# TensorE in program order through a first attention with no weight conversion beside it, and value blocks moved in the load queue

## The chip, the cores and the metric

One core of one Trainium2 chip runs the whole program. The metric is the device time of one execution in microseconds (us). Times of different kernels are compared only through runs of the same rounds on the same chip.

## The reference, cut to what matters

```python
# q, k, v: (4, 8, 768, 64) float32; two weights: 512 x 2048 and 2048 x 512
def _attn_ref(q, k, v):                       # block 32, window 16
    k_sum = k.reshape(B, H, nb, 32, D).max(axis=3)     # one key per block
    v_sum = v.reshape(B, H, nb, 32, D).mean(axis=3)    # one value per block
    # softmax over near keys (|i - j| < 16) and all block keys (+ log 32)
    ...
    return np.matmul(a, np.concatenate([v, v_sum], axis=2))

def _moe_ref(x, w_ch1, w_ch2):                # x: (4, 768, 512)
    mixed = np.real(np.fft.fft(np.fft.fft(x, axis=1), axis=2))
    u = x + mixed
    un = (u - u.mean(-1)) / np.sqrt(u.var(-1) + 1e-6)
    return u + np.maximum(un @ w_ch1, 0.0) @ w_ch2
```

Each of the four batches goes through attention (four pairs of heads), Fourier mixing, a norm, a hidden layer and an output layer. The two products with the weights are most of the work.

## The kernel before, where the change and the argument touch it

The weights arrive as 64-bit words, and VectorE and ScalarE turn them into float32 on the chip, one half matrix at a time. Each of the 16 matrices (w1 and w2, eight each) is needed first in batch 0, so all conversion lies in batch 0's time. The list `plan` says in which order matrices are converted, and from which stage on each may begin (`None` is at once, `fold` and `mx` are stages of the Fourier mixing).

```python
plan = [(1, 0, None), (1, 1, ("fold", 0)), (1, 2, ("mx", 0)), (2, 0, ("mx", 0)), (1, 3, ("h", 0, 0)), ...]

def convert(piece, dst):                      # one half of a matrix
    load_raw(i + 3)                           # loads run three pieces ahead
    nc.vector.tensor_scalar(out=ex, in0=high, ...bitwise_and)       # 2 of these, 0.42 us each
    nc.vector.tensor_scalar(out=man, in0=high, ...bitwise_and)
    nc.scalar.activation(out=ex, ...); nc.scalar.activation(out=tmp[:, 1, :], ...)
    nc.vector.scalar_tensor_tensor(out=ex, in0=high, ..., in1=ex, ...)   # 2 of these
    nc.vector.scalar_tensor_tensor(out=tmp[:, 1, :], in0=low, ..., in1=tmp[:, 1, :], ...)
    tt(dst, tmp[:, 1, :], tmp[:, 0, :], ALU.mult)                   # VectorE
    ...
def make(f, j):                               # two halves, then sums of quarters
    ...
    if f == 1:
        _left_sums(tt, ...)                   # 4 VectorE sums, for products of seven instead of eight
    else:
        to, wv = to[:, 0:4], wv[:, 0:4]       # w2: no sums in batch 0; batch 1 makes them on its first load
```

Block sums of the values are made from loads of their own, on GpSimd (`gtt`) or, for batch 1, on VectorE (`tt`). A load of the next half of a batch is issued together with the values of every second pair.

```python
def block_sums(b, gg):                        # 4 heads
    ...                                       # 4 loads of 192 KB
    add = tt if b == 1 else gtt
    add(raw[0], raw[0], raw[1], ADD)          # 6 operations on GpSimd, 4 on VectorE
    ...
def load_values(b, g):
    if g % 2 and following(b, g, 1):
        block_sums(*divmod((b * NP + g + 1) // 2, NP // 2))
    ...
def get_w2(b, j):                             # from batch 1 on
    if b == 1:
        fetch(out=w[:, 0:4], in_=dw2[j][:, 0:4])
        _right_sums(tt, lambda i: w[:, i])    # 4 VectorE sums
        fetch(out=dw2[j][:, 1:7], in_=w[:, 1:7])
```

In the output layer batch 0 uses plain products, the others seven products of half size in place of eight. In the fold at the start of the Fourier mixing, `keep_busy` lets TensorE multiply the fold's own tiles, which is meant to keep its clock up.

## Time and profile before

| | before |
|---|---|
| median of 3 runs (range) | 847.06 us (846.79 to 847.75) |
| profiled span, granted clock | 846.1 us, 0.988 |
| first hidden matmul, first output matmuls of batch 0 | 103.07, 152.44 us |
| second hidden half of batch 0 starts | 203.96 us |
| output of batch 0's second half | 63.42 us |

Two views of the kernel before: VectorE from the end of the norms (97.23 us) to the last w2 matrix of the first output (159.87 us), in which the columns are the stretch, its length, then busy us (and instructions) of PE, PEld, DVE, ACT and POOL, the granted clock, the DMA share and GB/s; and TensorE's waits from the first hidden matmul to the second half (engine, line and tile, what it waited for, us in total, times, longest).

```profile
97.23:159.87 62.64, 57.59 (x582) 33.99 (x580) 52.68 (x104) 41.27 (x79) 6.36 (x6) 1.00 0.81 232
```

### The profile page before, as it was taken

What the parts mean: (1) busy time and instruction counts of PE and PEld (TensorE: products, weight loads), DVE (VectorE), ACT (ScalarE), POOL (GpSimd) and SP (SyncE); (2) the same over time, 40 slices, a digit from 0 to 9 for tenths busy, and PEclk for the clock granted to TensorE, in tenths of its full rate; (3) what the DMA queues carried; (4) which work ended last, traced back from release to release, by engine and by line L of the source; (5) the groups of instructions that cost most, each with busy time, mean ns of one, the idle gap of its engine ahead of it and who ended that gap; (6) DMA issues with size and microseconds to landing.
All of it is one profiled execution on the core that took longest, in us unless ns stands there. A gap on an engine that the chain in (4) does not pass through costs nothing.

```text
span 846.1 us, 14497 instructions
## 1 busy us (share of the span) xinstructions
PE 813.9 (96%) x6006; PEld 569.1 (67%) x6006; DVE 479.4 (57%) x1115; ACT 230.5 (27%) x473; POOL 36.3 (4%) x44
## 2 busy tenths in 40 slices
PE   6979988999999999999999999999999999999997
PEld 5857655545556555787667875688667885786586
DVE  2588996986966443544357943443337952532352
ACT  3524756542721113122232104120321012101100
POOL 3200011003000200001000000000000000000000
PEclk9969999999999999999999999999999999999999
DMA  9997594979523274454843236403411326205001
GB/s 220 230 274 164 166 232 171 289 235 298 187 78 131 75 277 131 116 112 158 239 106 100 71 134 215 115 21 82 167 60 54 113 64 247 88 1 217 1 27 53
DMA packets 102858, 120.94 MB, mean 143 GB/s; under 512 B 50592, under 2 KB 83584, under 8 KB 102784
## 3 DMA queue, kind: packets, MB, share of 16 engines
q1 hardware_dynamic: 102240, 119.77, 48.6%
q8 instruction: 49, 0.80, 0.4%
q10 hardware_dynamic: 544, 0.17, 0.1%
q14 instruction: 25, 0.20, 0.1%
HBM read 95.80 MB, written 24.12 MB: 142 GB/s over the span
## 4 chain that ended last, share of the span: by engine, by line
PE 79%; DVE 10%; ACT 5%; DMA 3%; issue 1%; SPq 0%; ACTq 0%; DVEq 0%
PE hx L1101 18%; PE ox L1167 13%; PE o L1142 9%; PE hz L1101 9%; PE oz L1167 7%; PE hy L1101 4%; PE y L1014 3%; PE oy L1167 3%; DVE x L560 2%; PE sc L735 2%; PE mx L963 1%; ACT qt L678 1%; ACT kt L678 1%; PE sc L695 1%; PE unt L1079 1%
## 5 line engine op out<-in xcount | busy, mean ns | idle before, releaser
L1101 PE MATMUL hx<-u,w 128*128 128x384 f32 x512 | 186.1, 492 | 8.8 <-ACT h L1111 6.2
L1101 PEld LDWEIGHTS hx<-u,w 128*128 128x128 f32 x512 | 94.4, 190 | 75.5 <-ACT h L1111 9.4
L1101 PE MATMUL hz<-u,w 128*128 128x384 f32 x256 | 93.2, 486 | 0.0
L1142 PE MATMUL o<-w,h 128*128 128x512 f32 x192 | 84.9, 595 | 0.0
L1101 PEld LDWEIGHTS hz<-u,w 128*128 128x128 f32 x256 | 48.6, 190 | 33.9 <-ACT h L1118 0.2
L1167 PE MATMUL ox<-w,s 128*128 128x256 f32 x288 | 69.0, 381 | 0.4 <-DVE x L560 0.3
L1167 PE MATMUL oz<-w,s 128*128 128x256 f32 x288 | 68.7, 379 | 0.0
L1167 PE MATMUL ox<-w,h 128*128 128x256 f32 x288 | 66.9, 380 | 0.0
L1142 PEld LDWEIGHTS o<-w,h 128*128 128x128 f32 x192 | 35.7, 190 | 41.9 <-issue 39.9
L560 DVE TENSOR_TENSOR x<-ox,x 128x256 f32<-128x256 f32 x72 | 30.3, 423 | 55.7 <-PE ox L1167 55.7
L1167 PEld LDWEIGHTS ox<-w,h 128*128 128x128 f32 x288 | 54.4, 190 | 8.3
L1167 PEld LDWEIGHTS ox<-w,s 128*128 128x128 f32 x288 | 53.9, 190 | 8.4 <-DVE x L560 1.2
L1167 PEld LDWEIGHTS oz<-w,s 128*128 128x128 f32 x288 | 54.4, 190 | 7.2
L560 DVE TENSOR_TENSOR h<-hx,h 128x384 f32<-128x384 f32 x32 | 17.8, 556 | 71.3 <-PE hx L1101 71.3
L560 DVE TENSOR_TENSOR h<-hy,h 128x384 f32<-128x384 f32 x32 | 17.8, 556 | 57.2 <-PE hy L1101 54.0
L1111 ACT COPY h<-hx 128x384 f32<-128x384 f32 x32 | 15.3, 478 | 121.7 <-PE hx L1101 110.0
L1101 PE MATMUL hy<-u,w 128*128 128x384 f32 x128 | 46.5, 486 | 0.0
L1127 ACT ACTIVATE h<-hx 128x384 f32<-128x384 f32 x32 | 15.7, 491 | 79.3 <-PE hx L1101 79.3
L1014 PE MATMUL y<-fs,fold 128*128 128x193 f32 x192 | 37.1, 336 | 0.0
L679 DVE TENSOR_REDUCE km<-kt 128x24 f32<-128x768 f32 x16 | 15.2, 951 | 37.7 <-ACT kt L678 24.6
L1014 PEld LDWEIGHTS y<-fs,fold 128*128 128x128 f32 x192 | 31.1, 189 | 7.4 <-issue 6.0
L1101 PEld LDWEIGHTS hy<-u,w 128*128 128x128 f32 x128 | 24.3, 190 | 17.0
(125 smaller groups left out, 1104.1 us busy)
## 6 DMA issues: line engine op xcount, KB each, us to landing
w<-dw SPq DMA_DIRECT2D x40, 896.0 KB, 5.2
words<-in_moe_w_ch_dram SPq DMA_DIRECT2D x32, 512.0 KB, 6.5
vw<-in_v_dram SPq DMA_DIRECT2D x47, 192.0 KB, 5.7
dw<-w SPq DMA_DIRECT2D x8, 896.0 KB, 6.9
kn<-in_k_dram SPq DMA_DIRECT2D x16, 384.0 KB, 4.9
qn<-in_q_dram SPq DMA_DIRECT2D x16, 384.0 KB, 5.7
vb<-in_v_dram SPq DMA_DIRECT2D x32, 192.0 KB, 5.6
out_dram<-x SPq DMA_DIRECT2D x24, 256.0 KB, 2.5
```

The costliest lines, as they stand in the source:

```text
L560: nc.vector.tensor_tensor(out=out, in0=in0, in1=in1, op=op)
L678: nc.scalar.copy(out=dst[D * e:D * (e + 1), s:S:2], in_=ps[D * s:D * (s + 1)])
L679: nc.vector.tensor_reduce(out=km[:, 0:nb], in_=kt[:, W:W + S].rearrange("p (n f) -> p n f", f=BLOCK), op=ALU.max, axis=AX.X)
L695: nc.tensor.matmul(ps[e][0:WK, n - n0, :], kt[rows, QB * n:QB * n + WK], qt[rows, QB * n:QB * (n + 1)], start=True, stop=True)
L735: nc.tensor.matmul(ps[h][r:r + 64, i, :], kt[rows, o:o + 64], qt[rows, o:o + BLOCK], start=True, stop=True)
L963: nc.tensor.matmul(out, y[:, g], table, start=True, stop=last, skip_group_check=True)
L1014: nc.tensor.matmul(y, fgs[par][:, st, P * g:P * (g + 1)], fs[par][:, g % 2, st, :], start=(st == 0), stop=(st == HT - 1))
L1101: nc.tensor.matmul(ps, w[:, a, kk, :], u[:, r, kk, :], start=start and kk == 0, stop=stop and kk == 1, skip_group_check=True)
L1111: nc.scalar.copy(out=c11, in_=X)
L1127: nc.scalar.activation(out=c21, in_=X, func=AF.Relu)
L1142: nc.tensor.matmul(ps, h[:, n, hf, P * t:P * (t + 1)], wt[2, b, j][:, 2 * hf:2 * hf + 2, :], start=(n, hf) == (0, 0), stop=(n, hf) == (NC ...
L1167: nc.tensor.matmul(ps, left[a][:, n, :], wt[2, b, j][:, r, :], start=start and n == 0, stop=stop and n == NC - 1, skip_group_check=True)
```

## The change

The intent: TensorE's first attention should run without waits. Its instructions keep the order of the program; warm-up matmuls run before the first keys land; pair 0's blocks get loads of half the size; the blocks of pairs 2 and 3 are loaded behind the keys of pair 3; no weight is converted in the attention; ScalarE takes copies of the fold. Beside this, the second half of batch 0's output becomes seven products, and batch 1's first block sums go to GpSimd.

```diff
-    plan = [(1, 0, None), (1, 1, ("fold", 0)), (1, 2, ("mx", 0)), ...
+    plan = [(1, 0, ("fold", 0)), (1, 1, ("mx", 0)), (1, 2, ("mx", 0)), ...
-        add = tt if b == 1 else gtt
+        add = tt if (b, gg) == (1, 1) else gtt
...
-        if g % 2 and following(b, g, 1):
+        if g % 2 and following(b, g, 1) and (b, g) not in ((0, 1), (1, 1)):
             block_sums(...)
...                                            # gen_attention, after pair 0's values
+            if (b, g) == (0, 0):
+                block_sums(0, 1)
+                load_raw(2)
...                                            # make, get_w2, gen_out
-        else:
+        elif j < NC:
             to, wv = to[:, 0:4], wv[:, 0:4]
+        else:
+            _right_sums(tt, lambda i: wv[:, i])
-        if b == 1:
+        if b == 1 and j < NC:
             fetch(out=w[:, 0:4], in_=dw2[j][:, 0:4])
-        if b == 0:
+        if (b, c) == (0, 0):
...                                            # fold: three copies from VectorE to ScalarE
-            nc.vector.tensor_copy(out=zq[:, par], in_=zw[:, :, Q])
+            nc.scalar.copy(out=zq[:, par], in_=zw[:, :, Q])
...
+    for i in range(2):
+        nc.tensor.matmul(ps, zeros[:, 512:640], zeros[:, 0:512], start=True, stop=True)
...
-    drive((first(attn, 6), 1, 0))
+    with tc.manual_schedule(engines={mybir.EngineType.PE}):
+        drive((first(attn, 6), 1, 0))
+    block_sums(1, 1)                           # behind the Fourier mixing of batch 0
```

(Cut: the mask of 32 KB for one of 384 KB, the split of pair 0's and 1's blocks, details of the value loads.)

## The prediction

> **What bounds the kernel now.** I read the page first: TensorE is busy 96% of the span, and the chain that ended last is 79% PE, 10% DVE, 5% ACT, 3% DMA. So most of the span is matmul time, which this change touches in one place only. What can be won lies where TensorE waits or runs at half clock, so I asked for stretches of the first 105 us, then the timeline of the end of the first attention. In each stretch the columns are length, then busy us (and instructions) of PE, PEld, DVE, ACT and POOL, then the granted clock, the DMA share and GB/s.
>
> ```profile
> 12.50:15.00 2.50, 1.50 (x22) 0.74 (x19) 2.37 (x3) 1.35 (x4) 2.34 (x3) 1.00 1.29 214
> 15.00:17.50 2.50, 0.57 (x4) 0.36 (x5) 1.50 (x2) 0.16 (x1) 1.52 (x3) 0.87 1.15 276
> ...
> 45.00:50.00 5.00, 5.00 (x41) 3.30 (x39) 3.13 (x6) 1.92 (x2) 0.00 (x0) 0.76 1.05 401
> 50.00:54.00 4.00, 3.65 (x50) 2.75 (x48) 2.87 (x6) 0.87 (x2) 0.00 (x0) 0.50 1.09 344
> 54.00:58.00 4.00, 0.00 (x0) 0.00 (x0) 4.00 (x7) 0.00 (x0) 0.13 (x1) 0.50 1.36 159
> ```
>
> See three things: TensorE starves at 14 to 17 us, DMA is full (share over 1) all along, and the last pair runs at clock 0.50. The timeline tells who is waited for.
>
> ```profile
> 16.73 0.57 PE L709 MATMUL vs<-vbs,sel 96*32 96x64 f32 x4 [2.73 <-POOL vbs L563]
> 17.51 2.83 PE L668 MATMUL qk<-ident,kn 128*64 128x128 f32 x24 [0.20 <-DMA kn<-in_k_dram]
> ...
> 41.12 0.63 ACT L860 ACTIVATE words<-words 128x512 f32<-128x512 int32 x1 [0.26 <-DVE words L858]
> ...
> 54.92 0.65 DVE L864 SCALAR_TENSOR_TENSOR words<-words 128x512 f32<-128x512 uint32 x1
> 55.48 0.55 DVE L560 TENSOR_TENSOR x<-av,rec 128x384 f32<-128x384 f32 x1
> 55.95 0.68 DVE L560 TENSOR_TENSOR w<-words 128x512 f32<-128x512 f32 x1
> 56.55 1.75 DVE L560 TENSOR_TENSOR fold<-x 128x1536 f32<-128x1536 f32 x1
> 58.35 4.24 PE L952 MATMUL busy<-fold,ident 128*128 128x512 f32 x6 [4.38 <-DVE fold L560]
> ```
>
> Block sums on POOL and the second pair's keys end the first stall. Weight conversion (`words`, `w`) sits in VectorE's queue between the last pair and the fold, and in ScalarE's queue among the last pair's copies. After that TensorE is busy 0.9 to 1.0, but VectorE, converting weights, is busy 35.4 of 40 us from 60 to 100 and 47.1 of 56.9 us from 103 to 160.
>
> **What the Trainium skill says.** (1) "TensorE: Matmul & The Clock Gate", Part 1: half clock when cold, full after some 3.4 us of sustained work. The trace agrees: 0.50 from 47.55 to 61.2 us, and a 24-matmul transpose group takes 2.83 us at the start, 1.53 us at 27.23. (2) "SBUF — State Buffer", two separate sides: a VectorE operation with two SBUF inputs and a GpSimd operation that reads SBUF exclude each other. I take it as the price of moving sums to GpSimd; no line above isolates it. (3) "DMA: Bandwidth & Descriptors", small descriptors: they are slow. The trace agrees: a 288 KB block of `vw` in 256-byte rows lands in some 1.4 us, 512 KB of weights in 1.3 to 2.3.
>
> **The change part by part.** For what moves I compared the order of instructions on each engine in both programs.
>
> *Start.* Warm-up matmuls before the keys land (4.62 us): 48 transposing matmuls of pair 0 took 2.83 + 2.80 us; at full clock some 3.0. The keys' arrival and the free-running clock window leave about 1 us of that. The mask shrinks from 384 to 32 KB and pair 0's value blocks from 768 to 384 KB, so 736 KB fewer lie before pair 1's keys: at 0.2 to 0.25 MB/us, 3 to 3.7 us. They should land near 14 us, not 17.4. POOL's sums start with the blocks (10.1 to near 7.8 us) and end near 14.3, and the matmul that needs them now follows the key transposes. Pair 1's scores start near 19.5 instead of 23.03: **3.5 us**.
>
> *A new wait.* The blocks of pairs 2 and 3 now come behind the keys of pair 3. Counting landings as before (2 us per 384 KB of keys, 2.6 per 768 KB of blocks), they land near 31 us, and POOL's sums took 6.5 us: ready near 36. In the new TensorE order everything of pair 3 stands behind that matmul (before: 36.67 us). So the 3.5 us shrink to **about 0.5** here, with TensorE idle some 3 us.
>
> *The last pair.* Before, from 36.67 to the last `av` at 53.97 took 17.3 us, half of it at half clock and with `words` activations between copies. In the new order: transposes 3, `av` 1.6, scores 3.9, ScalarE's value copy and last exponential 2, last mask and `av` 1.5, waits about 1: 13 us, plus up to 3 if the clock falls in the idle gap. End near 50: **4 us** gained.
>
> *Fold.* Removed between the last `av` and the fold: two word operations and one product (0.6 us apart each, partly under the `x` writes): 1.3 us. Inside the fold, four `w` sums (0.35 apart) and six copies go away or to ScalarE: 2 us. The first half gains 5.6 us (62.37 to 56.8), the second 7.8. TensorE then runs `y` and `mx` back to back (idle 0.8 us of 25 before), so 5.6 is what passes: hidden layer at 97.4 instead of 103.07.
>
> *Conversion given back.* One w1 matrix costs 6.3 us of VectorE: per half 2 x 0.335 + 3 x 0.60 = 2.47 us by start-to-start times, plus four sums of 0.34. About 5.8 us of the first one was paid within the attention and now comes after it; the value sums of batch 1's first half (3 us) leave VectorE. Before, the last w2 matrix that the first output tile needs was ready at 159.87, when TensorE wanted it. By adding the new VectorE order from the norms on (38.6 us conversion, 20 us other, 3 us waits) I get 152 to 154, so the gain there is 6 to 8 us: **7**. VectorE has the room because before it idled some 10 us waiting for TensorE.
>
> *Output of batch 0's second half as seven products.* Rows removed: 96 of 128x512, 42.0 us. Added: 168 of 128x256 at 1.73/8 = 0.216 us: 36.3. Net 5.7 at best. Batch 1 does just this already and is the better measure:
>
> ```profile
> 240.36:303.78 63.42, 63.42 (x242) 36.59 (x241) 37.66 (x103) 8.73 (x24) 4.99 (x5) 1.00 0.29 97
> 441.11:500.93 59.82, 59.25 (x314) 50.13 (x313) 45.88 (x126) 8.23 (x22) 0.00 (x0) 1.00 0.30 80
> ```
>
> 3.6 us less for the stage; I take **3**, since only 5.2 us of output matmuls now stand before the `y` that needs the fold (8 in batch 1). The 16 added w2 sums (6.8 us of VectorE) come while the hidden layer runs (24.6 busy of 36.4) and should just fit. Batch 1 loses the same sums and four stores: **1**, as the chain passed through one such load and sum at 391 to 399 us.
>
> Sum: 7 + 3 + 1 = 11: 847 - 11 = 836.
>
> **The rivals.** *VectorE becomes the bound at 60 to 160 us.* Every weight is one place later; if copies and rectifiers queue behind it, TensorE waits 1.1 to 1.5 us at a time on hidden copies, as before (6.2 us in five waits). For: busy 35.4 of 40. Against: one matrix is 6 us, and the fold is 7.8 earlier. It would leave 3 us at the front: 840 to 843. *The late blocks cost more than the early keys give.* For: DMA is full, and the sums take 6.5 us on POOL in series. Against: before, pair 3 began no earlier for other reasons. With a cold clock behind it, 2 us less: 838 to 840. *Pair 3 runs warm and without a gap*: attention ends at 46.5, and the w2 matrices come at 150: 830 to 832. *All hidden*: the attention's gain is taken back by transfers of tables; they land by 53.4 us, so this is unlikely.
>
> **Range and chances.** The front holds the doubt: 3 to 11 us. The other 4 us are likely to 1.5. So 836, 8 times in 10 within 829 to 843. Faster by 2% means under 830.1: only if pair 3 and the conversion both go well, 0.14. Slower by 2% would take a stall of 28 us that nothing shows: 0.01.
>
> **What would show it.** Right: `sc` of pair 1 near 19.5; `vs` of pair 2 waits for POOL near 36; last `av` at 48.5 to 51.5; first hidden matmul at 95 to 99; the output stage 3 us shorter; everything after 310 us the same, shifted. Wrong: `hx` waiting on VectorE's `w` or long on ScalarE copies between 100 and 155, the last `av` later than 52, a cold clock past 61 us, or a gap before the batch-0 output because w2 sums are late.

## More of the kernel before

```profile
PE hx L1101 <- ACT h L1111: 3.9, 3, 1.5
PE av L772 <- DVE vs L560: 1.2, 1, 1.2
PE hx L1101 <- DVE h L560: 0.9, 1, 0.9
```

VectorE is busy 52.68 of 62.64 us, the rest is waiting.

## The result

| | before | after |
|---|---|---|
| median (range), 4 runs each | 846.92 us (846.19 to 847.75) | 846.27 us (845.34 to 848.04) |
| ratio after/before, 95% interval | | 0.9994 (0.9976 to 1.0013): the same |
| profiled span, granted clock | 846.1, 0.988 | 844.2, 0.994 |

A ratio here and below is the mean time of one kernel's runs over the mean of the other's of the same rounds, so it is not quite the ratio of the medians. The changed kernel ran three rounds more on another chip beside later experiments: 845.77 us, 0.9985 (0.9962 to 1.0009). The prediction of 836 us, with a range of 829 to 843, was wrong.

Where the time went is seen by the starts of stages on TensorE, read from both traces:

| stage starts at (us) | before | after | gained so far | gained as predicted |
|---|---|---|---|---|
| scores of pair 1 | 23.03 | 20.54 | 2.5 | 3.5 |
| last `av` of the attention ends | 53.97 | 51.42 | 2.6 | 4 |
| first hidden matmul | 103.07 | 97.63 | 5.4 | 5.6 |
| second hidden half of batch 0 | 203.96 | 206.23 | -2.3 | 7 |
| output of the second half | 240.36 | 242.63 | -2.3 | 7 |
| first hidden matmul of batch 1 | 303.78 | 301.89 | 1.9 | 10 |
| first output of batch 1 | 349.36 | 349.98 | -0.6 | 10 or 11 |
| end | 846.14 | 844.25 | 1.9 | 11 |

At the first hidden matmul the gain is nearly what was foreseen (some 2.2 us of it is work that only moved behind this point, see below; the norms end 4.2 us earlier). Two stages took it back: 7.7 us between 97 and 206 us, and 2.5 us in batch 1's first hidden half. The 2.5 us between the last two rows are gained in four later stages, 0.4 to 0.8 us in each; no run looks into them. The same two views of the changed kernel (its norms end at 92.98 us, the last w2 matrix is ready at 162.68), and the waits from its first hidden matmul to the second half:

```profile
92.98:162.68 69.70, 63.24 (x596) 37.24 (x596) 62.68 (x124) 42.84 (x82) 6.58 (x6) 0.98 0.87 237
```

```profile
PE hx L1111 <- DVE h L560: 3.2, 1, 3.2
PE av L778 <- DVE vs L560: 1.7, 1, 1.7
PE hx L1111 <- ACT h L1121: 1.2, 1, 1.2
PE o L1152 <- DVE w L560: 0.9, 1, 0.9
```

The stretch is 69.70 us long, not 62.64; VectorE is busy 62.68 of it. TensorE now waits for VectorE, 5.8 us in all, where it waited 2.1 us for VectorE and 3.9 for ScalarE. The timeline (start, us, engine, line, operation, out<-in, shape, count, idle time before it and what ended that) shows what VectorE did before the longest wait:

```profile
127.03 4.97 POOL L563 TENSOR_TENSOR vb_None<-vb_None,vb_None 96x512 f32<-96x512 f32 x3 [75.40 <-DMA vb_None<-in_v_dram]
...
129.38 1.49 DVE L864 TENSOR_SCALAR words<-words 128x512 int32<-128x512 int32 x1
130.78 1.50 DVE L865 TENSOR_SCALAR words<-words 128x512 int32<-128x512 int32 x1
...
135.59 1.56 PE L1111 MATMUL hx<-u,w 128*128 128x384 f32 x4 [3.16 <-DVE h L560]
```

Two word operations take 1.49 and 1.50 us while GpSimd adds blocks. The same operation takes 0.42 us elsewhere. The sum into `h` stands behind them in VectorE's queue, and TensorE waits 3.16 us for it.

The 7.7 us are not all waiting, though. TensorE from its first hidden matmul to the second half, before and after (columns as above):

```profile
103.07:203.96 100.89, 94.83 (x773) 50.60 (x771) 85.88 (x168) 53.48 (x99) 12.91 (x12) 1.00 0.83 243
97.63:206.23 108.60, 101.29 (x797) 54.46 (x791) 95.80 (x188) 55.82 (x105) 14.89 (x12) 0.98 0.84 240
```

Its idle time grew from 6.1 to 7.3 us; the other 6.5 us it is busy. Three things in the two traces make up 6.2 of them. Transposes and block scores of batch 1's attention, which took 2.2 us right before the first hidden matmul (100.92 to 103.07 us), now come right after it. The scores of one pair come in two groups some 6 us apart: 48 matmuls alone take as long as 96 together (1.59 us at 118.71, 1.60 at 169.00), and with the block scores this costs 2.4 us. And after the wait of 3.16 us the clock reads 0.50 from 137 to 140 us, which costs 1.6. The program fixes TensorE's order in the first attention only; why it came out otherwise here, no run tests. So the time at which the last w2 matrix is ready is the better measure of VectorE's queue.

The second loss, in batch 1, reads so:

```profile
309.96 1.55 DVE L560 TENSOR_TENSOR w<-w 128x256 f32<-128x256 f32 x4 [2.88 <-DMA w<-dw]
311.43 0.55 DVE L560 TENSOR_TENSOR h<-hx,h 128x384 f32<-128x384 f32 x1
...
312.04 1.24 PE L1111 MATMUL hx<-u,w 128*128 128x384 f32 x3 [2.24 <-DVE h L560]
```

VectorE stands 2.88 us waiting for a w2 matrix to come back from memory, to make its four sums. The sum into `h` that frees TensorE's bank is the next in its queue.

And the new wait of the attention, as the prediction had it:

```profile
37.21 0.41 PE L714 MATMUL vs<-vbs_None,sel 96*32 96x64 f32 x4 [2.39 <-POOL vbs_None L563]
```

### The profile page after: what moved, and what is told of

The parts are those of the page before. It is cut to its first block, busy times and chain, and to the rows that moved or that the text cites. A ratio compares the mean times of both kernels' runs of the same rounds, so it can differ in the third digit from the quotient of the medians.

```text
span 844.2 us, 14730 instructions
## 1 busy us (share of the span) xinstructions
PE 810.5 (96%) x6082; PEld 581.0 (69%) x6082; DVE 491.7 (58%) x1117; ACT 233.1 (28%) x497; POOL 50.9 (6%) x57
## 4 chain that ended last, share of the span: by engine, by line
PE 80%; DVE 9%; ACT 5%; DMA 3%; POOL 1%; issue 1%; SPq 0%; ACTq 0%; DVEq 0%; POOLq 0%
PE hx L1111 19%; PE ox L1175 16%; PE hz L1111 9%; PE oz L1175 8%; PE hy L1111 4%; PE oy L1175 4%; PE y L1024 4%; PE o L1152 3%; PE sc L740 2%; DVE x L560 2%; PE mx L972 2%; ACT qt L682 1%; ACT kt L682 1%; PE unt L1089 1%; PE ss L756 1%; DVE w L560 1%
## 5 line engine op out<-in xcount | busy, mean ns | idle before, releaser
L1175 PE MATMUL ox<-w,s 128*128 128x256 f32 x336 | 80.7, 381 | 0.3
L1175 PE MATMUL oz<-w,s 128*128 128x256 f32 x336 | 80.5, 379 | 0.0
L1175 PE MATMUL ox<-w,h 128*128 128x256 f32 x336 | 78.0, 380 | 0.0
L560 DVE TENSOR_TENSOR x<-ox,x 128x256 f32<-128x256 f32 x84 | 35.3, 422 | 61.1 <-PE ox L1175 61.0
L1175 PEld LDWEIGHTS ox<-w,h 128*128 128x128 f32 x336 | 63.4, 190 | 9.7
L1175 PEld LDWEIGHTS ox<-w,s 128*128 128x128 f32 x336 | 62.7, 190 | 9.5 <-DVE x L560 1.2
L1175 PEld LDWEIGHTS oz<-w,s 128*128 128x128 f32 x336 | 63.5, 190 | 8.4
L560 DVE TENSOR_TENSOR h<-hx,h 128x384 f32<-128x384 f32 x32 | 17.8, 556 | 66.8 <-PE hx L1111 66.8
L1152 PE MATMUL o<-w,h 128*128 128x512 f32 x96 | 42.4, 596 | 0.9 <-DVE w L560 0.9
L1175 PE MATMUL oy<-w,h 128*128 128x256 f32 x168 | 39.7, 379 | 0.0
```

The source lines that it names most:

```text
L560: nc.vector.tensor_tensor(out=out, in0=in0, in1=in1, op=op)
L1152: nc.tensor.matmul(ps, h[:, n, hf, P * t:P * (t + 1)], wt[2, b, j][:, 2 * hf:2 * hf + 2, :], start=(n, hf) == (0, 0), stop=(n, hf) == (NC ...
L1175: nc.tensor.matmul(ps, left[a][:, n, :], wt[2, b, j][:, r, :], start=start and n == 0, stop=stop and n == NC - 1, skip_group_check=True)
```

## The experiments

Eighteen kernels were run. Every one but two gives the right result; e17 and e19 are wrong. "Stretch" is the time from the first hidden matmul of batch 0 to its second hidden half, "idle" is TensorE's idle time in it, "w2" the time from the end of the norms to the last w2 matrix of the first output on VectorE, "batch 1" the time from its first hidden to its first output matmul; all are from the traces. The kernel before spread more on these chips (845.5 to 853.2 us) than in the first rounds, so differences under some 2 us are read from the stages. Nor is the start steady: in the other traces with the changed kernel's attention its last `av` ends between 49.8 (e16) and 53.3 us (e18).

| kernel | median us | ratio to before (95%) | first hidden at | stretch | idle | w2 | batch 1 |
|---|---|---|---|---|---|---|---|
| before (first trace) | 846.92 | 1 | 103.07 | 100.89 | 6.1 | 62.6 | 45.58 |
| changed (first trace) | 846.27 | 0.9994 (0.9976 to 1.0013) | 97.63 | 108.60 | 7.3 | 69.6 | 48.09 |
| e18 changed again | 845.77 | 0.9985 (0.9962 to 1.0009) | 99.49 | 106.99 | 7.3 | 68.0 | 47.09 |
| e1 conversion back | 852.34 | 1.0048 (1.0004 to 1.0091) | 109.73 | 102.36 | 5.9 | 64.6 | 47.29 |
| e7 e1, GpSimd quiet | 850.56 | 1.0043 (0.9999 to 1.0087) | 107.05 | 102.34 | 5.9 | 64.6 | 47.25 |
| e2 before, conversion late | 853.34 | 1.0065 (1.0019 to 1.0110) | 104.51 | 104.24 | 5.7 | 66.8 | 45.57 |
| e17 no first matrix | (845.20) | 0.9964 (0.9936 to 0.9991) | 99.65 | 107.56 | 7.8 | 70.0 | 47.16 |
| e19 e17, next one place earlier | (844.24) | 0.9962 (0.9921 to 1.0002) | 100.58 | 102.39 | 5.9 | 64.6 | 47.05 |
| e3 last block sums on GpSimd | 849.02 | 1.0006 (0.9968 to 1.0044) | 97.49 | 112.17 | 9.5 | 71.6 | 48.43 |
| e9 GpSimd's sums later | 843.45 | 0.9931 (0.9899 to 0.9963) | 97.80 | 103.13 | 2.5 | 62.8 | 51.41 |
| e16 e9, loads not moved | 846.38 | 0.9982 (0.9961 to 1.0003) | 95.68 | 110.36 | 6.9 | 69.2 | 49.72 |
| e14 before, GpSimd's sums later | 845.88 | 0.9976 (0.9947 to 1.0004) | 103.51 | 98.24 | 3.6 | 57.5 | 45.57 |
| e4 w2 sums on GpSimd | 844.44 | 0.9963 (0.9917 to 1.0009) | 98.72 | 107.00 | 7.3 | 68.0 | 45.66 |
| e6 before, seven products | 847.83 | 0.9982 (0.9936 to 1.0028) | 102.72 | 100.72 | 6.2 | 62.9 | 51.15 |
| e5 blocks ahead of keys | 843.87 | 0.9947 (0.9916 to 0.9977) | 95.47 | 108.62 | 7.3 | 68.0 | 47.34 |
| e11 other busy matmuls | 849.75 | 0.9997 (0.9958 to 1.0036) | 103.33 | 105.25 | 6.8 | 67.2 | 49.73 |
| e12 e9 and e4 | 838.73 | 0.9888 (0.9867 to 0.9908) | 97.91 | 102.77 | 2.3 | 62.8 | 45.62 |
| e13 e12, six busy matmuls | 836.47 | 0.9861 (0.9838 to 0.9884) | 95.78 | 102.90 | 2.4 | 62.8 | 45.60 |
| e15 e13 and e5 | 835.02 | 0.9856 (0.9834 to 0.9877) | 92.84 | 102.84 | 2.3 | 62.8 | 45.60 |
| e20 e15, two matrices at the fold | 839.22 | 0.9885 (0.9851 to 0.9919) | 100.43 | 100.29 | 1.8 | 62.7 | 45.60 |

### The moved conversion: e1, e7, e2, e17, e19

The first theory was that the conversion which left the attention used up the gain. e1 puts it back.

```diff
-    plan = [(1, 0, ("fold", 0)), (1, 1, ("mx", 0)), (1, 2, ...
+    plan = [(1, 0, None), (1, 1, ("fold", 0)), (1, 2, ...
```

> The changed kernel with one line undone: the first w1 matrix is converted within the first attention again, as in the kernel before. Theory (the moved conversion uses up the attention's gain, because VectorE's queue from the fold to the last w2 matrix of the first output is full): the fold and the first hidden matmul come 1 to 2 us later (98.6 to 99.6 instead of 97.63 us), but the last w2 matrix of the first output is ready near 157 instead of 162.67, the TensorE wait on h at 135.59 goes, batch 0's second hidden half starts 3 to 5 us earlier than 206.23, and the kernel takes 839 to 842 us. Rival (the loss at 100 to 160 us comes from somewhere else: GpSimd's sums[...], the value sums that moved to 117 us, the cold clock): the attention loses 1 to 2 us and nothing comes back, 845 to 848 us.

Both expectations missed: 852.34 us. The stretch did shrink, from 108.60 to 102.36 us, as the theory says. But the last `av` came at 61.04 us, 9.6 later than in the changed kernel. The timeline of e1 shows why:

```profile
43.71 4.61 POOL L563 TENSOR_TENSOR vb_None<-vb_None,vb_None 96x512 f32<-96x512 f32 x3
...
45.45 1.75 DVE L560 TENSOR_TENSOR w<-words 128x512 f32<-128x512 f32 x1
...
51.20 1.02 DVE L560 TENSOR_TENSOR x<-av,rec 128x384 f32<-128x384 f32 x2
51.90 0.39 PE L699 MATMUL sc<-qt,kt 64*96 64x64 f32 x1 [6.45 <-DVE x L560]
```

Conversion operations take 1.75 us beside GpSimd's block sums, 0.69 otherwise. The write of `x`, which frees a bank for TensorE, stands behind them, and TensorE waits 6.45 us. In the kernel before, this did not happen, because these sums were on VectorE. So the change's parts depend on each other: with the block sums on GpSimd, the conversion had to leave the attention. e7 checks this: as e1, with these sums on VectorE again.

```diff
-        add = tt if (b, gg) == (1, 1) else gtt
+        add = tt if b == 1 else gtt
```

> The changed kernel with the first w1 matrix converted within the first attention (as e1_conv_back), and with the block sums of batch 1's first half on VectorE as in the kernel before, so that GpSimd is quiet while VectorE converts. Theory (in e1_conv_back GpSimd's sums at 43 to 50 us made VectorE's conversion operations take 1.75 us instead of 0.68, and TensorE waited for a bank behind them): the last av of the first attention ends at 53 to 55 us instead of 61.04, the first hidden matmul comes at 100 to 103, batch 0's second hidden half at 200 to 204, and the kernel takes 841 to 846 us. Rival (VectorE's order, conversion ahead of the writes of x that free banks, does it alone): last av at 58 us or later, 849 us or more.

```profile
45.40 0.70 DVE L560 TENSOR_TENSOR w<-words 128x512 f32<-128x512 f32 x1
...
49.20 1.05 PE L699 MATMUL sc<-qt,kt 64*96 64x64 f32 x6 [3.04 <-DVE x L560]
```

The same operation takes 0.70 us again. From the scores of pair 1 to the last `av` it took 33.4 us, against 40.4 in e1 and 30.9 in the changed kernel: GpSimd made 7.0 of the 9.5 us, VectorE's order (the rival) the rest, with a wait of 3.04 us. By its absolute times (last `av` at 58.34 us, 850.56 us) the run lies in the rival's window, not the theory's; this run's pair 1 began 4.4 us later, after a wait for keys, so only the time from pair 1 on tells the two apart.

e2 takes the kernel before and moves the conversion alone.

```diff
-    plan = [(1, 0, None), (1, 1, ("fold", 0)), (1, 2, ...
+    plan = [(1, 0, ("fold", 0)), (1, 1, ("mx", 0)), (1, 2, ...
```

> The kernel before with one line of the change alone: the first w1 matrix is converted after the fold instead of within the attention. Theory: the last pair and the fold gain 1 to 2 us (first hidden matmul 101 to 102 instead of 103.07), the last w2 matrix of the first output comes some 5 to 6 us later than 159.87, TensorE waits for it, batch 0's second hidden half starts 3 to 6 us later than 203.96, and the kernel takes 849 to 853 us. Rival (VectorE has the room, as the prediction held): 844 to 847 us.

853.34 us, 5 to 6 more than before, just above the theory's window, and the traced end is 5.2 us later. The last w2 matrix comes 5.5 us later (165.40 us), 4.2 of them behind the norms. The early gain did not come: the first hidden matmul is at 104.51 us, not 101 to 102. The prediction's "VectorE has the room" is refuted in this kernel. TensorE does not show it as waiting: the stretch is 3.4 us longer with its idle time at 5.7 us, and 2.5 us of it go with a pair's scores that again come in two groups (119.25 and 123.12 us).

How much is it in the changed kernel? e17 leaves the first matrix out.

```diff
+        if (f, j) == (1, 0):
+            load_raw(4)
+            nc.gpsimd.memset(wv, 0.0)
-        for hh in range(2):
+        for hh in range(2 if (f, j) != (1, 0) else 0):
...                                            # and no left sums for it
```

> The changed kernel without the conversion of the first w1 matrix at all (GpSimd fills it with zeros: a wrong result on purpose). It measures what that conversion costs where the change has put it. Theory (VectorE's queue from the fold to the first output is full, so the 6.3 us of the conversion pass on): first hidden matmul 0 to 1.5 us earlier than 97.63, first output matmul of batch 0 at 149.5 to 152 instead of 155.65, batch 0's second hidden half at 200 to 202 instead of 206.23. Rival (the conversion fits into VectorE's waits at 65 to 76 us, and the loss is GpSimd's alone): first output matmul at 154.5 us or later.

The theory missed: a stretch of 107.56 us, no gain. The design was at fault: the place that was emptied, at 65 to 76 us, was one in which VectorE had time. The plan moved every matrix one place later, so the one that counts is the second, which now waits for the norms. e19 lets that one into the empty place.

```diff
-    plan = [(1, 0, ("fold", 0)), (1, 1, ("mx", 0)), ...
+    plan = [(1, 0, ("fold", 0)), (1, 1, ("fold", 0)), ...
```

> e17_no_first with one more edit: the second w1 matrix is let in at the fold, in the place that the first left empty, as in the kernel before, instead of after the norms (a wrong result on purpose still: the first matrix is zeros). e17 gained nothing, because it emptied a place at 65 to 76 us in which VectorE had room. Theory (the change moved every matrix one place later, so one more of them, 6.3 us, stands in VectorE's full queue between the norms and the first output): batch 0's second hidden half at 199 to 202 us instead of 206 to 207, 839 to 842 us. Rival (the number of matrices in that queue does not matter, GpSimd's sums do): 205 or later, 844 us or more.

The stretch is 102.39 us, 5.2 less than e17, of which 1.9 are idle time; the last w2 matrix is ready at 158.15 instead of 162.88 us, 5.4 nearer to the norms. The second half began at 202.97, a little later than expected, and the median of 844.24 us (841.88 to 847.95) missed the window of 839 to 842, so this rests on the trace. One matrix more in the queue behind the norms costs some 5 us there, in agreement with e1.

### GpSimd beside VectorE: e3, e9, e16, e14

e3 takes 3.05 us of block sums off VectorE (at 117 to 122 us) and gives them to GpSimd.

```diff
-        add = tt if (b, gg) == (1, 1) else gtt
+        add = gtt
```

> The changed kernel with the block sums of batch 1's second half on GpSimd instead of VectorE. Theory (VectorE's queue is the bound from 97 to 155 us; 3.05 us of it at 117 to 122 are these sums): they run on GpSimd at 75 to 85 us, the last w2 matrix of the first output is ready at 159 to 161 instead of 162.67, batch 0's second hidden half starts at 203 to 205 instead of 206.23, 843 to 845 us. Rival (GpSimd holds VectorE up as much as it takes from it): 845.5 to 848 us, with the norms later.

The rival was right, and more: the stretch grew to 112.17 us. The sums ran at 116 to 124 us, not at 75 to 85 as expected, so they too stood beside the conversion. Giving GpSimd this work there did not free VectorE.

e9 moves the block sums that GpSimd makes at 127 to 134 us, for batch 2, to the first output.

```diff
-        ... and (b, g) not in ((0, 1), (1, 1)):
+        ... and (b, g) not in ((0, 1), (1, 1), (1, 3)):
+                if t == 0:                     # gen_out, batch 0, first half
+                    block_sums(2, 0)
```

> The changed kernel with the block sums of batch 2's first half (GpSimd, 127 to 134 us) put off to the first output. Theory (GpSimd's sums make VectorE operations wait for memory in the stretch in which VectorE is the bound: two took 1.5 us instead of 0.42, one 0.95): VectorE gets 2 to 3 us back, the TensorE wait on h at 135.59 shrinks, batch 0's second hidden half starts at 203 to 205 instead of 206.23, 843 to 845 us. Rival (no share in it): within 1 us of the changed kernel at every stage, 845.5 to 847 us.

843.45 us, as expected, and the second half came at 200.93 us, earlier than expected. VectorE from the end of its norms to the last w2 matrix in e9 (columns as above):

```profile
93.10:155.99 62.89, 59.72 (x580) 34.98 (x581) 59.01 (x122) 42.65 (x82) 0.00 (x0) 1.00 0.90 255
```

With GpSimd at 0.00, VectorE is busy 59.01 us where it was 62.68, and waits 3.9 us instead of 7.0. The last w2 matrix comes at 155.99, 6.7 us earlier. TensorE's wait of 3.16 us is gone, and it is busy for all but 2.5 us of the stretch. The sums now ran at 172 to 180 us, in the first output, in which TensorE waits 0.4 us in all. (The 768 KB loaded for them moved too.)

e16 leaves the loads in place and lets the sums alone wait, for the last tile of the first hidden half.

```diff
+                    ins = nc.gpsimd.tensor_copy(out=gate, in_=h[:, NC - 1, 0, S - 1:S])
+                    with tc.issue_after(ins.ins):
+                        block_sums(2, 0, part=1)      # part=0, the loads, stays where it was
```

> e9_vb20_late put off both the loads (768 KB) and the GpSimd sums of batch 2's first half. Here the loads stay where the changed kernel has them and the sums alone wait, for the last tile of the first hidden half. Theory (it is GpSimd's sums beside VectorE): as e9_vb20_late, first output matmul at 151 to 153 us, TensorE's wait of 3.16 us for h gone. Rival (it is the loads that hold up the weights' loads): as the changed kernel, first output matmul at 155 to 156.5 us.

```profile
148.03 4.53 POOL L563 TENSOR_TENSOR vb_None<-vb_None,vb_None 96x512 f32<-96x512 f32 x3
148.28 1.75 DVE L560 TENSOR_TENSOR w<-words 128x512 f32<-128x512 f32 x1
...
149.96 1.48 DVE L872 TENSOR_SCALAR words<-words 128x512 int32<-128x512 int32 x1
...
155.62 1.13 PE L1159 MATMUL o<-w,h 128*128 128x512 f32 x2 [1.71 <-DVE w L560]
```

The first output matmul came at 149.36 us, earlier than the theory's 151 to 153 by the 2 us that this run's hidden layer began earlier, so the loads were not to blame. But the sums then ran at 148 to 155 us, beside the conversion of the last w2 matrices, slowed those to 1.75 and 1.48 us, and TensorE waited 3.4 us for them in the output. The stretch is no shorter than in the changed kernel. So the cost follows GpSimd's sums to wherever VectorE is the bound.

e14 makes the edit of e9 in the kernel before.

```diff
-        if g % 2 and following(b, g, 1):
+        if g % 2 and following(b, g, 1) and (b, g) != (1, 3):
+                if (c, t) == (0, 0):
+                    block_sums(2, 0)
```

> The kernel before with the block sums of batch 2's first half put off to the first output, as in e9_vb20_late. It tells whether GpSimd's sums at 123 to 131 us are a cost that both kernels had, or one that the change made. Theory (the kernel before had slack on VectorE there, the changed one has none): 0 to 1.5 us less, first output matmul of batch 0 at 153 to 155, 845 to 847 us. Rival (a cost in both): batch 0's second hidden half 3 us or more earlier than 203.96, 842 to 844 us.

845.88 us, 0.9976: within the theory's window. But the last w2 matrix comes 4.7 us earlier (155.16 us), 5.2 nearer to the norms; in the changed kernel the same edit gave 6.9 there (5.3 against its second trace). So for VectorE the cost was there before, at much the same size, as the rival had it. Less of it passed on: the second hidden half came 2.2 us earlier (the rival's 3 were not reached), in the changed kernel 5.3. e14 against e9 does not measure the moved matrix: they differ in the whole change, and in e9's longer stretch (103.13 to 98.24 us) TensorE is idle less.

### Batch 1's first hidden half: e4, e6

e4 gives the sums of batch 1's first four w2 matrices to GpSimd.

```diff
-            _right_sums(tt, lambda i: w[:, i])
+            _right_sums(gtt, lambda i: w[:, i])
```

> The changed kernel with the 16 sums of batch 1's first four w2 matrices on GpSimd instead of VectorE. Theory (in batch 1's first hidden half VectorE's queue, in order, holds the sum over h behind sums that wait for the w2 reload, which comes later behind the seven-product output): the TensorE wait of 2.24 us at 312.04 goes, the stage from the first hidden to the first output matmul of batch 1 takes 45.5 to 46.5 us instead of 48.09, and the kernel takes 841.5 to 843 us. Rival (the stage is longer for the values' and scores' waits of the next attention, or GpSimd's reads hold VectorE up as much): 843.5 to 846 us.

The stage takes 45.66 us, as in the kernel before (45.58), and one wait is left in TensorE's list for it, 1.1 us for ScalarE, which the kernel before also has. The median of 844.44 us is above the window, with the stretch unchanged. GpSimd's sums do no harm here, because VectorE has time.

e6 adds the seven products, and the sums that belong to them, to the kernel before.

```diff
-        if b == 0:
+        if (b, c) == (0, 0):                   # gen_out
-        if b == 1:
+        if b == 1 and j < NC:                  # get_w2
-        else:
+        elif j < NC:                           # make
             to, wv = to[:, 0:4], wv[:, 0:4]
+        else:
+            _right_sums(tt, lambda i: wv[:, i])
```

> The kernel before with one part of the change alone: the second half of batch 0's output as seven products, with the right sums of its w2 matrices in the conversion. Theory: that output stage takes 59 to 60 us instead of 63.42, batch 1's first hidden half gives 2 us of it back in a TensorE wait on h (as in the changed kernel), the stages before it are as in the kernel before, and the kernel takes 844 to 846 us. Rival 1 (nothing is given back): 842.5 to 843.5 us. Rival 2 (the 16 sums come in the way of the second hidden half): batch 0's second hidden half longer than 36.4 us, 847 us and over.

The output stage took 59.44 us, 4.0 less, and batch 1's first hidden half 51.15 us, 5.6 more: all was given back (847.83 us, the same). The expected loss was 2 us. The waits of this stage in e6 start with the same one; below it the stage in e6 and in the kernel before (columns as above):

```profile
PE hx L1103 <- DVE h L560: 2.1, 1, 2.1
```

```profile
299.28:350.43 51.15, 47.90 (x436) 29.45 (x434) 21.57 (x52) 13.42 (x28) 0.00 (x0) 0.93 0.63 198
303.78:349.36 45.58, 44.45 (x435) 27.43 (x434) 21.00 (x49) 13.43 (x28) 0.00 (x0) 1.00 0.62 196
```

The wait explains 2.1 of the 5.6 us. In the other 3.5 TensorE is busy, for 47.90 us instead of 44.45 with the same matmuls: the granted clock is 0.93, because it reads 0.50 from 311 to 317 us, right behind the wait. In e9, at 51.41 us, it is the same; in the changed kernel a wait of 2.24 us was followed by a clock of 1.00. All runs with e4's edit have 45.6 or 45.7 us, so wait and clock go with VectorE's w2 sums.

### The attention: e5, e11

e5 loads the blocks of pairs 2 and 3 ahead of the keys of pair 3, as before.

```diff
+            if (b, g) == (0, 0):
+                block_sums(0, 1)               # ahead of the loads of the keys
             for n in {(0, 1): (), ...
...
             if (b, g) == (0, 0):
-                block_sums(0, 1)
                 load_raw(2)
```

> The changed kernel with the value blocks of pairs 2 and 3 loaded ahead of the keys of pair 3, as in the kernel before, not behind them. Theory (the prediction's new wait): the TensorE wait of 2.39 us for GpSimd's sums at 37.21 goes and with it the half clock at 38 to 41.5 us, the keys come later by less than that, the last av ends at 48.5 to 50 us instead of 51.42, the first hidden matmul at 95 to 96.5; at the end 0 to 2 us less than the changed kernel. Rival (the keys then come too late by the same): last av at 51 to 53, no gain.

TensorE's list of waits for 25 to 50 us in e5 has no line of GpSimd's any more. The last `av` ends at 49.25 us, the first hidden matmul comes at 95.47, and the end at 843.87 us, ratio 0.9947. So the wait comes from loading the later blocks behind the keys. Its price, 2.2 us at the first hidden matmul, is not clear of the spread of the other traces (95.68 us in e16, without this edit), and the interval of the ratio overlaps that of e18.

e11 lets the matmuls that keep TensorE busy read a finished tile instead of the fold's.

```diff
+                for _ in range(13):            # behind the last av
+                    nc.tensor.matmul(ps, ident, p.rearrange(...)[:, 0:512], start=True, stop=True)
-        if (b, par) == (0, 0):                 # keep_busy
+        if False:
```

> The changed kernel with the matmuls that keep TensorE busy before the fold reading a finished tile right behind the last av, 13 of them, instead of the fold's own tiles. Theory: the clock stays at 1.00 through the fold, VectorE's waits of 0.97 and 0.54 us for them go, the fold ends at 63.5 to 64 instead of 65.4, the first hidden matmul comes at 95.3 to 96.3 instead of 97.63. What passes on to the end depends on VectorE, whose work also starts 1.5 us earlier: batch 0's second hidden half 1 to 2 us earlier, 844 to 845.5 us. Rival (clock falls anyway, or the y matmuls wait for VectorE just the same): first hidden matmul at 97 or later, 846 us or more.

It missed: the first hidden matmul came at 103.33 us. Six of the 13 were scheduled among the `y` matmuls, and the clock fell all the same. TensorE had stood still for 1.69 us before the last `av`, and its clock in e11 reads:

```profile
48.00:50.00 2.00, 0.33 (x4) 0.16 (x4) 1.75 (x2) 1.94 (x3) 1.84 (x3) 1.00 1.04 385
50.00:52.00 2.00, 1.91 (x46) 1.77 (x47) 0.56 (x1) 0.48 (x1) 0.37 (x2) 0.86 1.04 411
52.00:54.00 2.00, 2.00 (x10) 1.10 (x7) 1.66 (x5) 0.00 (x0) 0.14 (x1) 0.50 1.01 390
```

It is at 0.50 in a stretch in which TensorE is busy all the time.

### Together: e12, e13, e15, e20, and e18 as reference

e12 is the changed kernel with the edits of e9 and e4.

> The changed kernel with the edits of e9_vb20_late and e4_w2sums_gps together. Theory (two separate losses: GpSimd's sums beside VectorE at 127 to 134 us, and batch 1's w2 sums in VectorE's queue at 304 to 325 us): both come back, 2.5 to 5 us and 2.4 to 5.7 us, batch 0's second hidden half at 201 to 203, batch 1's first hidden half 45.5 to 46.5 us long, 836 to 840 us. Rival (the second loss takes up what the first gives, since all waits for the same queue of loads): 842 us or more.

838.73 us, 0.9888. Batch 1's loss comes back in full, and of the stretch's 7.7 us come back 5.8; in the rest TensorE is busy (100.5 us, idle 2.3).

e13 adds six busy matmuls of a finished tile (`range(6)` in e11's edit), so that none falls among the `y`.

> e12_w2gps_vb20 with six matmuls of a finished tile in place of those that read the fold's tiles. Theory: VectorE's two waits in the fold (1.5 us) go, no busy matmul lands among the y as in e11_static_busy, the first hidden matmul comes 1 to 2 us earlier than in e12_w2gps_vb20, and the kernel takes 1 us less than it. Rival (the clock has fallen by then and the y matmuls run at half clock): first hidden matmul the same or later, the same time.

836.47 us; the first hidden matmul comes 2.1 us earlier than in e12, 1.7 of them behind the last `av`. This run's clock stayed at 1.00 from 46 to 60 us.

e15 adds the edit of e5.

> e13_plus_busy with the value blocks of pairs 2 and 3 ahead of the keys of pair 3 (the edit of e5_early_blocks). Theory (the four losses are separate and their sum passes to the end): the last av 1.5 to 2.5 us earlier than in e13_plus_busy, the first hidden matmul at 93.5 to 94.5 us, the kernel 1.5 to 2.5 us less than e13_plus_busy: 834 to 835.5 us. Rival (VectorE, from the norms to the first output, has become the bound again): 836 to 837 us.

835.02 us, 0.9856 (0.9834 to 0.9877). It beats both kernels. Its trace ends 3.0 us before e13's; the medians differ by 1.5 us, and the ratios' intervals overlap. The page's first lines:

```profile
span 832.0 us, 14734 instructions
## 1 busy us (share of the span) xinstructions
PE 808.4 (97%) x6086; PEld 578.5 (70%) x6086; DVE 485.7 (58%) x1101; ACT 233.0 (28%) x497; POOL 60.0 (7%) x73
```

GpSimd works more here than before the change (60.0 us to 36.3), at times when VectorE is not the bound.

e20 lets the second w1 matrix in at the fold too (the edit of e19 on e15).

> e15_all_four with the second w1 matrix let in at the fold as well, behind the first. Theory: in VectorE's new order the second conversion stands between the x writes and the norms, so the first hidden matmul comes 3 to 6 us later than 92.84, and what the queue after the norms gains (up to 6.3 us) only pays it back: 834 to 838 us, no gain. Rival (VectorE has the room there): 830 to 833 us.

839.22 us: no mend. The first hidden matmul comes 7.6 us later, more than expected, as the conversion stands between the norms' operations, and the stretch gains only 2.6.

e18 is the changed kernel again, as reference on the same chip.

> The changed kernel once more, on the same chip and in the same rounds as the runs beside it, as the reference for them: 845.5 to 848 us, the stages within 1 us of the first trace.

845.77 us. Its stages are within 2 us of the first trace, not within 1: the first hidden matmul came 1.9 us later. TensorE waited 3.17 us for `h` here too, but the clock stayed at 1.00 behind it.

## Why the prediction was wrong, by its own steps

- **Start and new wait: right in kind.** Scores of pair 1 at 20.54 (19.5 foretold); the wait for GpSimd ended at 37.21 (36 foretold). The rival "the late blocks cost more than the early keys give" holds a part of the truth: e5 takes the wait away, and the clock read 0.51 behind it (38 to 41.5 us); the 2.2 us that e5 puts on it are within the spread of the traces. What the prediction reads as a cold start is read from durations alone: the clock record shows 1.00 at 5 to 10 us, where the transposes took 2.83 us. And the 1.4 and 1.3 to 2.3 us of its third note are the times between landings; from issue to landing the trace has 3.9 us or more.
- **Last pair and fold: nearly right, in part by luck.** Last `av` at 51.42 (48.5 to 51.5); first hidden matmul at 97.63 (97.4). But the first `y` came at 58.85, not 56.8: the fold gained 3.6 us and not 5.6, and the norms 4.2. The rest at the first hidden matmul is the 2.2 us of attention work that moved behind it, which the prediction did not have. VectorE waited 1.5 us inside the fold for the busy matmuls, which was not foreseen; e13 shows that this came back.
- **"Conversion given back", the gain of 7 at the first output: this step failed.** It added up VectorE's new order behind the norms: 38.6 of conversion, 20 of other work, 3 of waits, 61.6 in all. The trace has 62.68 busy and 7.0 of waits, 69.70. With GpSimd's sums out of the way (e9) it has 59.01 and 3.9, 62.89, so the sum was near the truth for a VectorE that is alone. The missing term is GpSimd's block sums at 127 to 134 us: 6.7 us of the time at which the last w2 matrix is ready, 3.9 to 5.5 us of the stretch. Of the 7.0 us of waits 4.3 are for TensorE's products; e9 has none of these. The 159.87 us that the prediction started from held the cost too (e14: 4.7 us). The prediction had the mechanism in hand as its second note from the Trainium skill, and priced it at nothing. Each duration came from an instruction without GpSimd beside it.
- **"VectorE has the room because before it idled some 10 us": failed beside GpSimd's sums, and open without them.** One more matrix behind the norms makes the way to the last w2 matrix 4.2 us (e2), 5.4 (e17 against e19) and 3.4 to 5.0 (the changed kernel's two traces against e1) longer. VectorE's busy time grows by 7 to 8 us in each, so a quarter to a half of the matrix did go into waits, not all of it. Without the sums, e20 takes a matrix out of e15's queue and the way stays at 62.7 us (62.8), but there TensorE is busy for all but 1.8 and 2.3 us of the stretch, so this does not show what VectorE alone could take. Undoing either cause in the changed kernel (e9, e1) took the stretch from 107 to 109 us down to 102 to 103.
- **Rival "VectorE becomes the bound at 60 to 160 us": right in its direction**, though its 840 to 843 us were too low, since it too left GpSimd out.
- **Output as seven products, 3: right.** 4.2 us in the trace.
- **Batch 1, a gain of 1: the sign was wrong.** The kernel lost 2.5 us there. The prediction counted fewer sums and stores, not when the remaining four matrices come back. In the trace they come later relative to the stage than before, and VectorE waits for them in order: the second matrix's sums begin 8.1 us into the stage instead of 2.5. e4 takes the loss away. That the seven-product output frees the w2 buffers later is the likely reason, since e6 shows the same loss with that part alone; when exactly each buffer came free was not tested.
- **Chances and range.** The doubt was put at 3 to 11 us for the front. It came out at -2.3, below both ends, as the two failed terms fall together. With GpSimd's sums moved and the w2 sums on GpSimd (e12), the change is worth 0.9888 of the time before, which is 9.5 us of 848.

What stays open: how much of e15's 1.5 us over e13 is real, why TensorE's order behind the attention differs between the kernels (some 2.4 us of scores in two groups), and whether VectorE has room for the moved matrix where GpSimd is quiet.

## What to carry to other kernels

A queue in which one engine is the bound cannot be added up from durations measured alone: look which other engine will run beside it in the new order, and take the slowed durations. Idle time of an engine is only room if the work can reach it; ask which gate each piece waits for, because moving the first piece of a list moves all of them. Measure a queue by when its last piece is ready, since the work of other engines can move across a stage's border. And work for an idle engine is free only where its neighbour isn't the bound: in the changed kernel the same GpSimd sums delay the last w2 matrix by 6.7 us at 127 us, and at 172 us TensorE waits no more than 0.4 us in the stage.

## What the Trainium skill lacked or had wrong

- "SBUF — State Buffer", section "Who interferes with whom": it says that a VectorE operation with two SBUF inputs contends with a GpSimd operation that reads SBUF, and that `tensor_scalar` can contend in its faster mode. The traces agree: 0.69 to 1.75 us for the one (e1, 45.45 us), 0.42 to 1.49 us for the other (129.38 us). It does not say what a stretch of such sums costs. Here 6.6 us of GpSimd sums cost VectorE 3.7 us of busy time and 3.1 us of waits, and up to 5.5 us of TensorE's time.
- The same page, section "Summary: rules for kernel authors", advises to schedule whichever of the two is off the critical path. The runs add when that is not enough: no engine waited for the result of batch 2's block sums at 127 us, and moving them by 20 us (e16) only moved the cost; moving them by 45 us (e9) removed it.
- "TensorE: Matmul & The Clock Gate", Part 1: it describes the fall of the clock as following an idle window of some 3.4 us, with free-running windows. In e11 TensorE's longest gap there was 1.69 us, and the clock still read 0.50 at 52 to 54 us, while TensorE was busy; in e13 a similar gap left it at 1.00. A wait of 2.12 us in e6 was followed by 6 us at 0.50, one of 2.24 us in the changed kernel by 1.00; one of 3.16 us and one of 3.17, in two traces of the same kernel, by 0.50 and by 1.00. So gaps under the window were followed by half clock in some traces and not in others, and the loss fell on the work after the gap.
- No page treats the order in which a freed buffer's reload and an unrelated bank's release meet in one in-order VectorE queue (2.88 us of VectorE's waiting for the reload before 309.96 us, and then 2.24 us of TensorE's before 312.04).
